# Block 1's second-half filter spectra from dense tables instead of two staged transforms, fewer guard matmuls, and a new written-out order

## The chip, the cores and the metric

The kernel runs on one core of a Trainium2 chip. The metric is the device time of one execution in microseconds (us); lower is better. The kernel before takes 278.72 us, the median of three runs (278.42 to 279.31).

## The reference

Two layers in a row on a sequence of 2048 positions with 640 channels. The first is a gated long convolution: the keys pass a short filter of four taps, are multiplied by the values, and the product is convolved along the sequence with a filter as long as the sequence. The second is a SwiGLU feed-forward layer.

```python
def _A_ref(q, k, v, shift_k, ssm_k, ssm_D):
    k_shift = sum(k_pad[:, t:t + S, :] * shift_k[:, ks - 1 - t] for t in range(ks))
    kv = k_shift * v
    y = irfft(rfft(kv, 2 * S) * rfft(ssm_k, 2 * S))[:, :S]      # per channel, causal
    y = y + kv * ssm_D
    return q * y

def _B_ref(x, w_gate, w_up, w_down):
    return (silu(x @ w_gate) * (x @ w_up)) @ w_down              # 640 -> 1728 -> 640

h = A_q + _A_ref(layernorm(A_q), A_k, A_v, A_shift_k, A_ssm_k, A_ssm_D)
out = h + _B_ref(layernorm(h), B_w_gate, B_w_up, B_w_down)
```

## The kernel before, in words

The sequence is cut into four blocks of 512 positions (j = 0 to 3), and the 640 channels into two column halves of 320 (c = 0 and 1). The convolution is done block by block through spectra of 1024 points. For each block and half the kernel needs a spectrum of the data (X) and a spectrum of the filter piece (K); products of these spectra are summed over the pairs of blocks that contribute, and the sum goes back to positions.

A spectrum is made in one of two ways.

- **Staged** (`fwd` at L659 and `spec` at L741): a first stage of 4 groups of 2 matmuls, 320 columns each, with 128x128 tables from the tile `tab` (names s1...); 4 evacuations by ScalarE (e1...); 4 transfers on SyncE's queue that exchange partitions (sh...); then a second stage of 4 groups (h = 0 to 3) of 4 small matmuls each, on a quarter of the array (64 by 64), which work side by side in pairs (s2...); and 4 more evacuations (e2...).
- **Dense** (`dense_h` at L689): 4 groups of 8 full matmuls of 320 columns with tables from the tile `den` (df...), and 4 evacuations (de...), with no transfer between.

Block 0 is all dense. Of the later blocks the set `DFW` says which spectra are dense: before, only the filter of block 1 in the first half, `("K",1,0)`. The dense tables lie in SBUF where the weights of the down projection (`wd`, and its last half tile `wdl`) are loaded later.

After the convolution of a block, VectorE and ScalarE form h (w..., h...), GpSimd takes the root of the variances (L878), the normed rows (hn...) are transposed (for block 0 by TensorE at L1143, names tr; for the others by DMA), and the feed-forward layer of that block runs on TensorE: gate and up (gu..., 5 matmuls of 512 or 256 columns in a group), silu on ScalarE (si..., L1198), a product on VectorE (gm...), and down (dn..., dl...) with the residual sum on VectorE (fa..., L1270 or L1251) and the store.

Nothing but data binds the order of the blocks: the feed-forward matmuls of one block fill TensorE while VectorE does the spectral products of the next (L751: m1, m2 products, ac sums, cr and ci combinations, kf filter sums, kvn, kva, kvv for the short filter). **The order is written out.** A packed table `_PLAN` gives for each operation its engine, its place in that engine's queue, its buffer slot, and extra ordering between transfers. `Prog.plan` reads it and `Prog.emit` issues each engine's list with semaphore waits where data or a buffer demands one. Each engine works strictly down its list, so an instruction that waits holds all behind it. All loads and exchanges but three stand in SyncE's one list.

TensorE also gets **guard matmuls**, on constant data and read by no one: `WARM` gives two sets (before, 5 and 4 matmuls of 512 columns) and `FILL` pairs of two (before, four pairs). Before, the first set and one pair stand at the very start; the second set and three pairs stand where block 0's convolution ends.

The tile `vin` holds the values of one block and half, loaded by SyncE into a single slot and multiplied in place (kvv). The key product of block 3's second half, kvv31, needs its load, vin31.

Of the kernel before, what the change touches and what calls it, by code (L numbers as in the profile page):

```python
# [317 lines left out]
def bass_sequential_preLN__ssm_conv_h3__swiglu_ffn__prompt_kernel(  # L318
# [20 lines left out]
    WARM = [5, 4]  # L339
    FILL = [2] * 4  # L340
# [10 lines left out]
    DFW = {("K",1,0)}  # L351
    KDMA = [[False, False], [True, True], [True, True], [True, True]]
    FM = 1664
# [12 lines left out]
    P = Prog()  # L366
    with ExitStack() as es:
# [335 lines left out]
        nks, dens = {}, []  # L703
# [603 lines left out]
        for j in range(NB):  # L1307
            block_j(j)

# [11 lines left out]
    "c-rlI2Y3@#*7m)URjgt)%a$$4vTRw!mYZa`$yS$Txy!v5Y~vDo?=28IgoIu~htL8E9YP=>VPPSmgiauY7FrT|Xd&ORu)z>^zukTIdv^cl&&)HPnS0MY=RNOv@67OUML<MEa39#c6H&`XfCINX+BPEc_y>2~x)a)6"  # L1321
    "wL~Gb`hOnb^*Fe-mGHvyAH92i{l~xmnTUiJ*%DqEMQpWeY4iAp_t!Vvn#aHI?)kMxyIw-OxPR~ZU)Mo<Cfgq`vwm5d*X#89*nicY@In!UKUn{7xc*!4zT_0U`S$o5t^a?j=kHa?<8Si*CjS3c-@nJx|CJK|+jIO!"
    ")JynNz5m2B=AVDc{O6yG|5upXbMDc4ys7n%Z&<>=;rexDwMBXv@t<!YxWCZ|?Y?AMGHLlPBOx;UB_bWPCZJ@L<nAZCEf~;FN1kBgfmn!wxQK>0h>5%r8!1tW`<ezle#i&$kT3FwRu8vN3Zla934U6xX>i2=Pi*7`"
    "KDcm2g^?T>>5ur(#sH7LNPt9ec*7omBq$ICAt89>BN+-oa-?#%MnTj-WJDI|jYWw_inPcE{>k8v<+k>OcyvG{1pjQXm4Qt#;1i%Q6p6x-23mZfUyUMAG>QS=L2x8M-g;z!D8Udb8JUp@S-~a}rJ)QM<v>obPeti~"
    "AQR=HY?OrxQ2}IEipo(1j7>&4C?6H0BEV9Ks==QD_Hgjdhmjia)WWR^+RWfN2Rvnfhg?8!L^Y@mT2r9c?)KpVFLsoN21Bm}Vq0NPK|Nqp2I_!1LhLFu3DBgWX4C}8I-vJaH`E1nLT|x+Bl-Z90fri|DuJu9s5|P9"
    "`haZ@v;^Acp^@kvGzLvXyHIB|9F0R0z}sgqdNO(!O-0kt9@G^LLPOCA7`qvKQh`|?U{nnC5<$KEfX!fFO#(HE0*+fynjnKA5VIO`DFPo9sHzuKfD0po-Qy%k0UiS2N(?oTLmd>btAL|u$T$yb5s%`arX`R=Eo9LE"
    "kz0^Az+FAy&I7ARsCNsS^^lhl_C#Q(GwKO=yP;lyc>rLpgNoEbO)`PY9^hjE^eu#*zUV`+T;$F}3Xwx0o)#iTf%c=_(e-d254q?;D{4Tf1e-AT-vl_T;Oqp}Gog0<&_K{Y1|W$=!+@#Y;Qehh3XKL<djq1*P^A*!"
    "p#n6L1tW$7<K<A<SnxCk7#|6ok4Nvh`R)nK_k!vbgO&zEotA@#rQme{S_9dyL@UrLXdj3^hB|D7{2IYq16qqdaYx<)ir)_Ynjk_m`Uq@WdKRF?=w~z&YW*QxO-6IkMew@>Z3Ej`VDl?jEQ0!f0m}Ip{RUND4+_`~"
    "u{IzAo&)v^(R@(Fd+01+`5Y866TJQoEf}9hKcGwK3X<Uk=rB5pj-ivt8_z|j&>3_NeUAe1eDqgz03AdpkPrR<W?KyK8w)Ha0^4ffqZ|}l3reYiOnac|z`?tqm<teb9iUu`p2CdQfvw#=GrB<KTjom|%oi8%nd?@*"
# [81 lines left out]
```

## Time and profile before

| | before |
|---|---|
| median of three runs | 278.72 us |
| the profiled execution, its own time | 278.8 us |
| its span, first to last instruction | 277.0 us |
| TensorE busy | 270.7 us, 98% |
| VectorE busy | 227.1 us, 82% |
| ScalarE busy | 196.7 us, 71% |
| DMA, mean over the span | 148 GB/s |

Times below are microseconds from the start of the span. PE is TensorE's matmul, PEld its weight loads, DVE is VectorE, ACT ScalarE, POOL GpSimd, SP SyncE (SPq its transfer issues). Ends of matmuls are modelled and overlap the next one's start, so the price of a matmul is taken from start to start. A bracket at the end of a row gives the idle time of the engine before it and what ended it.

### The profile page before, as it was taken

How to read it: one execution, taken by the hardware profiler on the slowest of the kernel's cores; microseconds unless marked ns; L12 is line 12 of the kernel's file. 1: busy time of each engine (PE TensorE's matmuls, PEld its weight loads, DVE VectorE, ACT ScalarE, POOL GpSimd, SP SyncE). 2: the span in 40 equal slices, each digit the busy share in tenths (PEclk: the TensorE clock that was granted, in tenths of full speed). 3: DMA queues.
4: the chain of work that ended last, by engine and by line, in shares of the span. 5: the costliest groups of instructions: out<-in, count | busy, mean ns of one | idle time of the engine just before them, and what ended most of it. 6: DMA issues, size and time to landing. Idle time of an engine off the chain costs nothing.

```text
span 277.0 us, 4869 instructions
## 1 busy us (share of the span) xinstructions
PE 270.7 (98%) x1761; PEld 149.3 (54%) x1761; DVE 227.1 (82%) x420; ACT 196.7 (71%) x319; POOL 13.1 (5%) x21
## 2 busy tenths in 40 slices
PE   8999999999999999999999999999999999999995
PEld 3676666454643575544444666444445766444573
DVE  3999999999999999999999998999997553015414
ACT  3479869999999988769998887879998730620000
POOL 1000200200001002000001011000001020000000
PEclk9999999999999999999999999999999999999999
DMA  6959969999889554665522645562021133000003
GB/s 191 282 162 294 223 178 262 271 225 300 294 244 252 198 142 122 193 211 146 164 68 80 193 133 140 161 200 84 23 74 55 50 62 106 12 0 0 0 14 107
DMA packets 54573, 40.97 MB, mean 148 GB/s; under 512 B 20243, under 2 KB 51732, under 8 KB 54550
## 3 DMA queue, kind: packets, MB, share of 16 engines
q1 hardware_dynamic: 54402, 40.63, 51.4%
q8 instruction: 14, 0.23, 0.3%
q14 instruction: 9, 0.07, 0.1%
q10 hardware_dynamic: 148, 0.04, 0.1%
HBM read 19.42 MB, written 2.62 MB: 80 GB/s over the span
## 4 chain that ended last, share of the span: by engine, by line
PE 50%; DVE 26%; ACT 8%; DMA 6%; SPq 4%; issue 3%; POOL 1%; DVEq 0%; ACTq 0%
PE ps L519 50%; DVE sb L751 23%; SPq L507 4%; DMA sb<-in_A_k_dram 3%; ACT sb L499 3%; DMA sb<-in_A_v_dram 2%; ACT sb L1097 1%; ACT sb L1198 1%; DMA sb<-sb 1%; POOL stt L878 1%; ACT sb L914 1%; DVE sb L1101 1%; DVE sb L1270 1%; ACT L1198 0%; ACT sb L893 0%
## 5 line engine op out<-in xcount | busy, mean ns | idle before, releaser
L519 PE MATMUL ps<-sb 128*128 128x320 bf16 (+3 forms) x1309 | 231.3, 332 | 1.5 <-DVE sb L533 1.1
L751 DVE TENSOR_TENSOR sb<-sb 128x1280 bf16<-128x1280 bf16 (+5 forms) x264 | 174.1, 721 | 2.4 <-DMA sb<-in_A_v_dram 1.0
L519 PEld LDWEIGHTS ps<-sb 128*128 128x128 bf16 (+2 forms) x1309 | 122.3, 98 | 96.0 <-issue 10.8
L499 ACT ACTIVATE sb<-ps 128x640 bf16<-128x640 f32 (+2 forms) x157 | 110.0, 755 | 24.7 <-PE ps L519 21.1
L519 PE MATMUL ps<-sb,tab 128*64 128x320 bf16 (+2 forms) x408 | 50.6, 302 | 1.9 <-DMA sb<-sb 0.8
L1198 ACT ACTIVATE sb<-ps 128x1024 bf16<-128x1024 f32 (+2 forms) x32 | 28.9, 918 | 19.3 <-PE ps L519 18.9
L519 PEld LDWEIGHTS ps<-sb,tab 128*64 128x64 f16 (+2 forms) x408 | 23.8, 101 | 26.6 <-issue 11.6
L751 DVE TENSOR_TENSOR sb<-ps,sb 128x1024 bf16<-128x1024 f32 (+3 forms) x18 | 15.8, 891 | 19.9 <-ACT sb L1198 15.4
L878 POOL TENSOR_TENSOR stt<-stt 128x2 f32<-128x2 f32 (+1 forms) x12 | 12.2, 1015 | 212.0 <-DVE stt L877 171.3
L1101 DVE SCALAR_TENSOR_TENSOR sb<-sb,stt 128x320 bf16<-128x320 bf16 x32 | 16.8, 543 | 5.5 <-ACT sb L1097 5.3
L1097 ACT ACTIVATE sb<-ps,stt 128x320 f32<-128x320 f32 x32 | 18.1, 619 | 4.3 <-PE ps L519 3.5
L921 ACT ACTIVATE sb<-sb,stt 128x640 uint8<-128x640 bf16 x16 | 13.2, 828 | 0.7 <-DVE stt L917 0.6
L1251 DVE SCALAR_TENSOR_TENSOR sb<-ps,stt,sb 128x320 bf16<-128x320 f32 x8 | 3.9, 546 | 10.4 <-PE ps L519 10.3
L1270 DVE SCALAR_TENSOR_TENSOR sb<-ps,stt,sb 128x640 bf16<-128x640 f32 x12 | 10.3, 877 | 2.5 <-PE ps L519 2.5
L914 ACT ACTIVATE sb<-sb 128x640 uint8<-128x640 bf16 x16 | 11.8, 735 | 0.3
L939 ACT ACTIVATE sb<-sb,stt 128x640 uint8<-128x640 bf16 x12 | 9.9, 826 | 0.9 <-DVE stt L934 0.7
L893 ACT ACTIVATE sb<-sb,stt 128x640 bf16<-128x640 bf16 x8 | 7.2, 914 | 0.7 <-DVE stt L885 0.7
L861 DVE BATCH_NORM_STATS2 stt<-sb 128x6 f32<-128x320 bf16 x8 | 3.8, 482 | 0.0
L892 DVE TENSOR_SCALAR sb<-sb,stt 128x640 bf16<-128x640 bf16 x8 | 3.4, 441 | 0.3 <-PE ps L1143 0.2
L500 DVE CAST sb<-ps 128x640 bf16<-128x640 f32 x1 | 0.8, 825 | 3.1 <-PE ps L519 3.1
L646 PE MATMUL ps<-sb 128*128 128x128 bf16 (+1 forms) x24 | 3.2, 226 | 0.0
L921 ACT ACTIVATION_READ_ACCUMULATOR sb<-sb,stt 128x1 f32 x16 | 3.1, 196 | 0.0
(24 smaller groups left out, 23.3 us busy)
## 6 DMA issues: line engine op xcount, KB each, us to landing
sb<-sb SPq DMA_DIRECT2D x68, 160.0 KB, 2.9
sb<-in_A_k_dram SPq DMA_DIRECT2D x6, 560.0 KB, 4.7
sb<-in_A_v_dram SPq DMA_DIRECT2D x8, 320.0 KB, 4.1
sb<-in_A_q_dram SPq DMA_DIRECT2D x8, 320.0 KB, 3.5
sb<-cst_den SPq DMA_DIRECT2D x8, 256.0 KB, 4.1
sb<-sb SPq DMA_DIRECT2D x24, 80.0 KB, 2.5
out_dram<-sb SPq DMA_DIRECT2D x12, 160.0 KB, 2.0
sb<-in_B_w_down_dram SPq DMA_DIRECT2D x3, 480.0 KB, 5.1
```

The source lines that it names most:

```text
L499: fns = {"act": lambda a: a.activation(out=dst(), in_=src(), func=ACTF.Copy), "dve": lambda v: v.tensor_copy(out=dst(), in_=src())}
L507: fns = [(lambda g, d=d, s=s: g.dma_start(d(), s())) for d, s in subs]
L519: return lambda t: t.matmul(o(), l(), r(), start=st, stop=sp)
L751: return lambda v: v.tensor_tensor(out=o(), in0=a(), in1=b_(), op=op)
L878: P.op({"pool": 1.05}, lambda g: g.tensor_tensor(out=y, in0=va, in1=stt[:, oCO + 4:oCO + 4 + hi - lo], op=ALU.pow), c1 + [(ST, "half")], c ...
L914: P.op({"act": act_c(D) + 0.22}, lambda a, b=b, jt=jt: a.activation(out=JU(jt), in_=V(xt, b * D, D), func=ACTF.Copy, accum_out=tmv(l, j, 4 ...
L921: P.op({"act": act_c(D) + 0.3}, lambda a, b=b, jt=jt: a.activation(out=JU(jt), in_=V(xt, b * D, D), func=ACTF.Square, bias=tmv(l, j, 5)[:, ...
L939: P.op({"act": act_c(D) + 0.3}, lambda a, b=b, jt=jt: a.activation(out=JU(jt), in_=V(xt, b * D, D), func=ACTF.Square, bias=tmv(l, j, 5)[:, ...
L1097: P.op({"act": act_c(CW, True)}, lambda a, k=k, b=b, wt=wt: a.activation(out=VF(wt, CW), in_=B32(pt, k, CW), func=ACTF.Identity, scale=tmv ...
L1101: vec(dve1(CW), lambda v, b=b, wt=wt, xv=xv: v.scalar_tensor_tensor(out=xv(), in0=xv(), scalar=tmv(0, j, 5)[:, b:b + 1], in1=VF(wt, CW), o ...
L1198: P.op({"act": act_c(n)}, lambda a: a.activation(out=dst(), in_=src(), func=ACTF.Silu), rd, wr, -1000, name=f"si{j}{i}")
L1270: vec(dve1(640), lambda v: v.scalar_tensor_tensor(out=hv(), in0=B32x2(pt, CW), scalar=tmv(0, j, 5)[:, b:b + 1], in1=hv(), op0=ALU.subtract ...
```

## The change

Three things change. The filter of block 1's second half becomes dense too; the second guard set (4 matmuls) and two of the four guard pairs go; and `_PLAN` is a new table, so that nearly every queue has a new order. A loop is added that makes the loads `wd` and `wdl` wait for every dense matmul of blocks 0 and 1, since these read the tables that lie where those weights go.

```diff
-    WARM = [5, 4]
-    FILL = [2] * 4
+    WARM = [5, 0]
+    FILL = [2] * 2
...
-    DFW = {("K",1,0)}
+    DFW = {("K",1,0),("K",1,1)}
...
         for j in range(NB):
             block_j(j)
+        for o in P.ops:
+            if o.name in ("wd", "wdl"):
+                for d in dens:
+                    if d not in o.deps:
+                        o.deps[d] = 2
+                        d.succ.append(o)
+                        o.npred += 1
...
 _PLAN = (
-    "c-rlI2Y3@#*7m)URjgt)%a$$4vTRw!mYZa`$yS$Txy!v5Y~vDo?=28IgoIu~htL8E9YP=>VPPSmgiauY7FrT|Xd&ORu)z>^zukTIdv^cl&&)HPnS0MY=RNOv@67OUML<MEa39#c6H&`XfCINX+BPEc_y>2~x)a)6"
...
+    "c-rlI2Xs@%y7i1?S(2?{HCvWt6-$<7xk|Dv*(z4CY{|CVd&9V!-a{y%*H8i>5J(7w4xt7@XbAyQfDj111_FfMLJ6JlJ_{2ZC-?pL-al)-`_{`j>zp%Z%2)Q@b2MHI1Vlsx&xJiF5w#q+-G!ju>z_Pv>q%%+YOzo7"
```

The engines' lists differ in these operations. TensorE loses 8 first-stage matmuls, 16 small second-stage matmuls and 8 guard matmuls of 512 columns, and gains 32 dense ones, so the count stays at 1761. ScalarE loses the four evacuations of the first stage. SyncE loses four exchanges. Two operations change engine, both from VectorE to ScalarE: the first evacuation of the taps at the start (L500 before), and one normed row of block 2 (hn23, L892 before, L893 now).

The first place is on TensorE, at the end of block 0's convolution. Before, from the last 8 inverse matmuls of block 0 (the first 8 of row 32; its other 24 are three dense groups of the first half's filter) to the first of the two transposes at L1143. `sb,tab 64x320` are second-stage groups, `sb,tab 128x320` first-stage matmuls, `sb 128x512` guards:

```order
32 L519 MATMUL ps<-sb 128x320 x32
33 L519 MATMUL ps<-sb,tab 128x320 x4
34 L519 MATMUL ps<-sb,tab 64x320 x4
35 L519 MATMUL ps<-sb,tab 128x320 x2
36 L519 MATMUL ps<-sb,tab 64x320 x4
37 L519 MATMUL ps<-sb 128x512 x4
38 L519 MATMUL ps<-sb,tab 64x320 x8
39 L519 MATMUL ps<-sb,tab 128x320 x2
40 L519 MATMUL ps<-sb 128x512 x2
41 L519 MATMUL ps<-sb,tab 64x320 x4
42 L1143 MATMUL ps<-sb 128x128 x10
```

Of the change, the same place; the last 8 inverse matmuls are the third group of eight in row 30, with dense groups before and behind them, and rows 32, 34, 36 and 39 are dense groups:

```order
30 L519 MATMUL ps<-sb 128x320 x40
31 L519 MATMUL ps<-sb,tab 64x320 x8
32 L519 MATMUL ps<-sb 128x320 x8
33 L519 MATMUL ps<-sb,tab 64x320 x8
34 L519 MATMUL ps<-sb 128x320 x8
35 L519 MATMUL ps<-sb,tab 64x320 x4
36 L519 MATMUL ps<-sb 128x320 x8
37 L519 MATMUL ps<-sb 128x512 x2
38 L1143 MATMUL ps<-sb 128x128 x10
39 L519 MATMUL ps<-sb 128x320 x16
40 L1143 MATMUL ps<-sb 128x128 x10
```

Dense groups of eight now stand between the second-stage groups and between the two transposes, where guards and first-stage matmuls stood.

The second place is block 3's filter in the first half. On SyncE, before, from a 64x512 transfer of block 1 (the only one there) to the load of vin31 (`in_A_v_dram`); `128x1x640` are exchanges, `32x4x320` pieces of the next filter:

```order
114 L507 DMA sb<-sb 64x512
115 L507 DMA sb<-sb 128x1x640
116 L507 DMA sb<-sb 32x4x320
117 L507 DMA sb<-sb 128x1x640
118 L507 DMA sb<-in_A_v_dram 128x4x320
```

Now, from the same transfer to the same load:

```order
110 L507 DMA sb<-sb 64x512
111 L507 DMA sb<-sb 32x4x320
112 L507 DMA sb<-sb 128x1x640
113 L507 DMA sb<-sb 32x4x320
114 L507 DMA sb<-sb 128x1x640
115 L507 DMA sb<-sb 32x4x320
116 L507 DMA sb<-sb 128x1x640 x4
117 L507 DMA sb<-sb 32x4x320
118 L507 DMA sb<-in_A_v_dram 128x4x320
```

Row 117 of before, and rows 114 and 116 of now but for one transfer, are exchanges of that filter; the load stood behind one of them, and now stands behind all four and seven transfers in all, counted from row 114.

On TensorE at that place, before, `sb,tab 128x320` are the filter's four first-stage pairs (row 123, row 125, the last two of row 129) and inverse matmuls, the others down projections of block 1:

```order
122 L519 MATMUL ps<-sb 128x320 x10
123 L519 MATMUL ps<-sb,tab 128x320 x2
124 L519 MATMUL ps<-sb 128x320 x10
125 L519 MATMUL ps<-sb,tab 128x320 x4
126 L519 MATMUL ps<-sb 128x320 x6
127 L519 MATMUL ps<-sb,tab 128x320 x4
128 L519 MATMUL ps<-sb 128x320 x10
129 L519 MATMUL ps<-sb,tab 128x320 x6
```

Now the four pairs are rows 119 and 121:

```order
118 L519 MATMUL ps<-sb 128x320 x10
119 L519 MATMUL ps<-sb,tab 128x320 x4
120 L519 MATMUL ps<-sb 128x320 x10
121 L519 MATMUL ps<-sb,tab 128x320 x4
122 L519 MATMUL ps<-sb 128x320 x6
```

The filter's last pair now ends 28 matmuls behind the start of that first down group, and stood 52 behind it before.

The third place is on VectorE, where kvv31 stands. Before it is row 199; the row behind it is hn23:

```order
195 L1270 SCALAR_TENSOR_TENSOR sb<-ps,stt,sb 128x640
196 L751 TENSOR_TENSOR sb<-sb 128x1280
197 L885 TENSOR_TENSOR stt<-stt 128x2
198 L877 TENSOR_SCALAR stt<-stt 128x2
199 L751 TENSOR_TENSOR sb<-sb 128x1280
200 L892 TENSOR_SCALAR sb<-sb,stt 128x640
```

Now kvv31 is the first of row 200:

```order
192 L1270 SCALAR_TENSOR_TENSOR sb<-ps,stt,sb 128x640
193 L877 TENSOR_SCALAR stt<-stt 128x2
194 L751 TENSOR_TENSOR sb<-sb 128x1280 x2
195 L885 TENSOR_TENSOR stt<-stt 128x2
196 L1270 SCALAR_TENSOR_TENSOR sb<-ps,stt,sb 128x640
197 L877 TENSOR_SCALAR stt<-stt 128x2
198 L751 TENSOR_TENSOR sb<-sb 128x1280 x2
199 L885 TENSOR_TENSOR stt<-stt 128x2
200 L751 TENSOR_TENSOR sb<-sb 128x1280 x4
```

Three products of 1280 columns (one in row 194, both in row 198) that stood behind kvv31 now stand ahead of it.

More of the change, by code (lines that the diff above doesn't have):

```diff
@@ new lines @@
+    "*m?29t@rj9q4h-n!rP1TAMgJ&9tpo?OZeR=Vr##aI<J5FY=7X^JpQ`37iF(Dt%Npy|GV<PuY<Now!L0u{fe9RJhdPD@AfDBrU=3xdjF@z^$I)e!PV;@)c)U8$$!U^*FVJl&+z|8ZGVlW{~yKuZ_e>=_5Qoe{$n=&"
+    ")vwH7`~CY*in%T3Uai-k)&B99l<*gn+bip(r&k{T^&0HS`em*!E@JEYiv%YbT6FM^k+)}EMuU1^M1@`?#DG>7@<AL#M?B<*WYCiiHNJ?6{Go<}1c(o{ULJd7M1gS>u+wt-K-m}W3>fE+0>LiLQ)YR_(V@&nLZ}yk"
+    "1s0U~C<v@c;Lb)|BuAl0ft1iHLt12kvK6HuDKa1j^ofBuS|VqHJuX;l@#+Jm7C%B1g2JFr2nqmODinbtQ5@Lg!Fx1{La|5#?J}^fM~Ns28KI99yqS<0B_kX3jzMWC6RA-;a>IyJ<b*LUl!0<l4k|?X;JFx;qH-8-"
```

114 lines of the change are left out of this document (55 added, 59 removed).

## The prediction

> **What bounds the kernel now.** I read the page's busy shares first, then its slices, to see which engines have room, and where.
>
> ```profile
> PE 270.7 (98%) x1761; PEld 149.3 (54%) x1761; DVE 227.1 (82%) x420; ACT 196.7 (71%) x319; POOL 13.1 (5%) x21
> ...
> PE   8999999999999999999999999999999999999995
> ...
> DVE  3999999999999999999999998999997553015414
> ACT  3479869999999988769998887879998730620000
> ```
>
> PE is busy in every slice (each is a fortieth of the span, 6.9 us). DVE is as full as PE in the slices from the second to the thirtieth and then empties. So the share of 82% misleads: it is an average over a full stretch and an empty one. The stretches show it in us:
>
> ```profile
> 14.50:211.00 196.50, 194.10 (x1275) 104.03 (x1273) 193.41 (x357) 172.52 (x285) 9.38 (x9) 1.00 0.62 176
> ```
>
> In the 196.5 us from 14.5 to 211 PE is busy for 194.10 and DVE for 193.41 (first and third of the busy columns). PE idles 2.4 us there and DVE 3.1 us. **Two engines work down their lists side by side**, and either can hold the other. After 211:
>
> ```profile
> 211.00:277.00 66.00, 63.15 (x413) 37.68 (x411) 24.32 (x52) 17.99 (x29) 2.77 (x3) 1.00 0.15 43
> ```
>
> Here PE has 413 matmuls left and DVE is idle for two thirds. This last stretch is PE's own, and its end moves with the time at which PE gets to it. A change is worth what both lists lose ahead of 211, and where they lose unequally, the smaller of the two.
>
> Which short waits set the pace before 211? For that I looked for idle brackets on PE and DVE in the timeline.
>
> ```profile
> 43.20 4.52 PE L519 MATMUL ps<-sb 128*128 128x320 bf16 x32
> ...
> 47.55 0.71 PE L519 MATMUL ps<-sb,tab 128*128 128x320 bf16 x4
> ...
> 49.11 1.23 PE L519 MATMUL ps<-sb,tab 128*64 128x320 bf16 x10 [0.85 <-DMA sb<-sb]
> ...
> 63.90 0.46 PE L519 MATMUL ps<-sb,tab 128*64 128x320 bf16 x4 [0.47 <-ACT sb L1198]
> 64.29 1.25 PE L519 MATMUL ps<-sb 128*128 128x512 bf16 x5
> ...
> 65.29 0.82 DVE L751 TENSOR_TENSOR sb<-sb 128x1280 bf16<-128x1280 bf16 x1 [0.27 <-ACT sb L499]
> 65.40 0.43 PE L519 MATMUL ps<-sb,tab 128*128 128x320 bf16 x2
> ...
> 167.83 0.82 DVE L751 TENSOR_TENSOR sb<-sb 128x1280 bf16<-128x1280 bf16 x1 [0.95 <-DMA sb<-in_A_v_dram]
> 168.69 0.45 DVE L892 TENSOR_SCALAR sb<-sb,stt 128x640 bf16<-128x640 bf16 x1
> ...
> 168.71 0.72 PE L519 MATMUL ps<-sb,tab 128*128 128x320 bf16 x4 [0.45 <-DVE sb L751]
> ```
>
> PE waits 0.85 us for an exchange of block 1's second half, 0.47 for a silu that must free its PSUM, and 0.45 for kvv31, which itself waits 0.95 us on DVE for the load vin31. That is 1.77 of PE's 2.4 idle us.
>
> **The change, part by part.** The sum is made against the profiled execution, 278.8 us for a span of 277.0; the 1.8 us around the span are not touched. The median, 278.72, lies 0.1 below it.
>
> *PE's work.* A full matmul of 320 columns costs (47.55 - 43.20) / 32 = 0.136 us, one of 512 columns (65.40 - 64.29) / 5 = 0.22 us. A second-stage group of four, from 63.90 to 64.29, costs 0.39: two pairs side by side, 2 x 0.136 = 0.27, and 0.12 for the way back to full matmuls. Added: 32 x 0.136 = 4.35. Removed: 8 first-stage matmuls, 1.09; four groups of small ones, 4 x 0.27 = 1.09; 8 guards, 8 x 0.22 = 1.76. That alone is **+0.41 us**. But PE's list now has 20 stretches of small matmuls where it had 24. The way in costs little more:
>
> ```profile
> 72.80 1.24 PE L519 MATMUL ps<-sb 128*128 128x512 bf16 x5
> 73.97 0.81 PE L519 MATMUL ps<-sb,tab 128*64 128x320 bf16 x8
> ```
>
> Five matmuls of 512 took 1.17 ahead of small ones and 1.11 ahead of full ones, so 0.06. Four stretches fewer save 4 x 0.18 = 0.72, between nothing (if the new neighbours cost as much) and that. I take all of it, as the nearest rows have it. PE's own work: **-0.3 us**, bounds -0.3 and +0.4.
>
> *PE's waits at the first place.* The 0.85 us wait goes: at 49.11 PE had run out of dense groups, and now four more groups of eight (4.35 us) stand among the second-stage groups and the transposes. The 0.47 us wait for silu goes too, because ACT was the late engine there:
>
> ```profile
> 43.00:66.00 23.00, 21.69 (x154) 11.70 (x153) 22.41 (x45) 22.41 (x36) 1.45 (x2) 1.00 1.03 263
> ...
> 150.00:176.00 26.00, 25.33 (x190) 15.40 (x189) 24.36 (x52) 22.12 (x38) 2.77 (x3) 1.00 0.54 146
> ```
>
> ACT was busy for 22.41 of these 23 us (fourth busy column), and four first-stage evacuations leave it:
>
> ```profile
> 161.42 0.69 ACT L499 ACTIVATE sb<-ps 128x640 bf16<-128x640 f32 x1
> ...
> 166.84 0.92 ACT L893 ACTIVATE sb<-sb,stt 128x640 bf16<-128x640 bf16 x1
> ```
>
> 4 x 0.69 = 2.8 us is six times the wait. Late next is the normed row for the first transpose:
>
> ```profile
> 51.47 0.80 DVE L892 TENSOR_SCALAR sb<-sb,stt 128x640 bf16<-128x640 bf16 x2
> ```
>
> From the last inverse matmuls (done by about 44.3: the first 8 of the 32 at 43.20) to the end of these two norms, 52.3, the chain took 8.0 us. PE's new list holds 5 dense groups, 5 small ones and a guard pair in between, 5 x 1.09 + 5 x 0.27 + 0.44 = 7.2 us and its turns. So up to 0.8 us of the 0.85 can come back as a wait for DVE; then DVE's list decides, which is counted next.
>
> *DVE's list.* It loses hn23, 0.45 us (the row at 168.69). ACT takes it at 0.92 (the row at 166.84), in a stretch where it is free for 3.9 of 26 us, and the transfer behind it is wanted by the feed-forward of block 2 only. DVE loses the tap evacuation too, but ahead of waits that stay:
>
> ```profile
> 4.80 0.82 DVE L500 CAST sb<-ps 128x640 bf16<-128x640 f32 x1 [3.12 <-PE ps L519]
> 5.81 4.57 DVE L751 TENSOR_TENSOR sb<-sb 128x2560 bf16<-128x2560 bf16 x4 [0.18 <-DMA sb<-in_A_k_dram]
> ...
> 14.56 1.89 DVE L751 TENSOR_TENSOR sb<-sb 128x2560 bf16<-128x2560 bf16 x2 [0.66 <-DMA sb<-in_A_k_dram]
> ```
>
> The load of the keys ends both waits, so **0** there (at most 0.18). Up to 14.56 the new list does the same work, and from there DVE is full. The 0.27 us wait at 65.29 was for a second-stage evacuation of the first half; its group now stands ahead of the transposes, so it goes. The 0.95 us for vin31 is the large one. The load was issued behind one exchange:
>
> ```profile
> 162.14 0.54 SPq L507 DMA_DIRECT2D sb<-sb  x1
> 162.79 0.58 SPq L507 DMA_DIRECT2D sb<-in_A_v_dram  x1
> ...
> 169.05 1.55 DVE L751 TENSOR_TENSOR sb<-sb 128x1280 bf16<-128x1280 bf16 x2
> ```
>
> That exchange waited for the filter's last first-stage evacuation, 161.42 to 162.11 on ACT; the load came at 162.79 and kvv31 ran at 167.83, 5.04 us later. Now the filter's last pair ends 28 matmuls behind the first down group and not 52, so 24 x 0.136 = 3.3 us earlier, and the evacuation ends near 158.8. Seven transfers of about 0.6 us follow, 158.8 + 4.3 = 163.1; but the table also makes SyncE hold the load until the fourth of them, an exchange of 160 KB, has landed, 2.9 us by its row below: 158.8 + 3 x 0.62 + 2.9 = 163.6, and data 5.04 later, 168.6. On DVE three products, 3 x 0.78 = 2.3 us, now stand ahead of kvv31, so that it is wanted not at 167.83 - 0.95 = 166.9 but near 169, with the 0.27 off. The load is there about 0.4 us early, and the wait goes. DVE's list ahead of 211: 0.45 + 0.27 + 0.95 = **1.67 us** less. PE's first stage of that half waits for kvv31, and its 0.45 goes with it.
>
> *SyncE's list.* Four exchanges go (0.6 us of issue each). The new waits of `wd` and `wdl` hold that queue once: one `wdl` load stands ahead of the pieces of block 2's filter and now waits for the last dense group, between the two transposes, near 55. The rows of exchanges and of such pieces on the page:
>
> ```profile
> sb<-sb SPq DMA_DIRECT2D x68, 160.0 KB, 2.9
> ...
> sb<-sb SPq DMA_DIRECT2D x24, 80.0 KB, 2.5
> ```
>
> Four of them issue in 2.4 us and land 2.5 later, near 61; PE's list has 40 matmuls of 512 and 30 of 256 columns, 40 x 0.22 + 30 x 0.11 = 12 us, between the second transpose and the first use, so near 67. Cost **0**; without that cover it would be what the issue is late beyond 6 us.
>
> *The guards.* In no stretch above does the granted clock fall below 1.00 (the column ahead of the DMA share), and PE idles 1.3 us in all between 43 and 66. At the start PE does run at half pace:
>
> ```profile
> 1.46 0.15 PEld L519 LDWEIGHTS ps<-sb 128*128 128x128 bf16 x1 [0.28 <-issue]
> 1.88 0.15 PEld L519 LDWEIGHTS ps<-sb 128*128 128x128 bf16 x1 [0.28 <-issue]
> ...
> 4.87 0.13 PEld L519 LDWEIGHTS ps<-sb 128*128 128x128 bf16 x1 [0.16 <-issue]
> 5.16 0.12 PEld L519 LDWEIGHTS ps<-sb 128*128 128x128 bf16 x1 [0.16 <-issue]
> ```
>
> A guard takes 0.42 us there, not 0.22, and a tap matmul of 320 columns 0.29 at 4.87, not 0.136. These first guards stay. Those that go stood between real matmuls, and dense matmuls take their place, so I cost their loss at nothing; the cover is that PE stays fed. [...]
>
> *The sum.* PE could gain 0.3 + 0.85 + 0.47 + 0.45 = 2.1 us, DVE 1.67. Both lists are full up to 211, so the smaller counts: 1.67. Of that I give back 0.3 for waits that a new order brings of its own. The old order has such:
>
> ```profile
> 97.29 0.55 DVE L1101 SCALAR_TENSOR_TENSOR sb<-sb,stt 128x320 bf16<-128x320 bf16 x1 [0.34 <-ACT sb L1097]
> ...
> 164.12 0.88 DVE L1270 SCALAR_TENSOR_TENSOR sb<-ps,stt,sb 128x640 bf16<-128x640 f32 x1 [0.33 <-PE ps L519]
> ```
>
> One of this size is what I add. **1.4 us less: 278.8 - 1.4 = 277.4 for the profiled execution, 277.3 us for the median.**
>
> **The rivals.**
>
> *The waits change place only.* DVE's waits come back elsewhere, vin31's or another of its size: the gain is hn23 and the 0.27, 0.7 us, so 278.0. For it: PE and DVE are so close that any late step costs both. Against it: each of the four waits named has lost its cause.
>
> *The load vin31 comes late; slower.* In the new list it stands behind all four exchanges of the filter. If the filter's last evacuation ends not near 158.8 but as late as before, at 162.1, the load is issued at 162.1 + 1.9 + 2.9 = 166.9, and kvv31 runs at 171.9. In the old list, with the three products ahead of it, it would have run at 167.83 + 2.3 = 170.1. That is 1.8 late, less the 0.7 gained: 278.7 + 1.1 = 279.8. It decides for slower once that evacuation ends after about 161.8. For it: seven more places in the queue. Against it: 24 matmuls less ahead of the evacuation.
>
> *The clock falls at the first place.* If PE drops to half pace there for as long as at the start (by the rows at least from 1.46 to 5.16, 3.7 us; I take 4.5), half of that is lost: 277.3 + 2.3 = 279.6. [...]
>
> *The dense spectrum does not pay and nothing else moves.* Then PE's own work counts, +0.4 at most: 279.1.
>
> **How the numbers follow.** A run of this kernel can be told from no change at about 0.3%, 0.84 us. My forecast, 277.3, has a chance of 0.58; its own range is from 276.4 (PE's whole 2.1 us and a little of its small waits) to 277.9. The waits that change place, 278.0, have 0.20; the late load, 279.8, 0.12; the clock, 279.6, 0.03; no gain, 279.1, 0.07. The range goes from 276.1, for the rest of PE's 2.4 idle us, to 279.5, which leaves out the late load, the clock, and a few in a hundred below. Faster by over 0.3% (under 277.9) are the forecast but for its edge and a little of the first rival: 0.59. Within 0.3% lie most of the first rival and the case of no gain: 0.26. Slower: 0.15.
>
> **What would show it.** Right: no bracket over 0.3 on PE between 43 and 66 and none near 168; the load from in_A_v_dram near 163.6 and DVE without a wait for it; in the stretch to 211 DVE idle for about 2 us and PE's tail of 66 us unchanged in length. Wrong: a PE wait for a norm (L892) ahead of the first transpose that is longer than 0.8; matmuls of 320 columns at more than 0.136 us in a stretch around 50; DVE idle for 3 us or more before 211, with new releasers. If DVE's idle time fell and PE still ended as late, the claim that the smaller gain counts would be wrong.

## The result, and the profile after

The changed kernel takes **281.64 us** (median of four runs, 280.85 to 283.11) where before took 278.70 beside it: a ratio of 1.0117 with a 95% interval of 1.0089 to 1.0145, so it is slower by 2.9 us. Two later sets of runs gave 282.49 us (ratio 1.0147, 1.0123 to 1.0171) and 282.19 us (1.0129, 1.0099 to 1.0158). The forecast was 277.3.

The profiled execution took 280.85 us, the fastest of the four, with a span of 279.0. First the page's busy shares and two stretches. Sixteen matmul records are missing (x1745 of 1761), so PE's busy time is too low by some 2 us; the weight loads (PEld) are complete.

```profile
PE 268.3 (96%) x1745; PEld 150.8 (54%) x1761; DVE 226.4 (81%) x418; ACT 195.3 (70%) x317; POOL 14.0 (5%) x21
...
q8 instruction: 14, 0.23, 0.4%
q14 instruction: 9, 0.07, 0.1%
```

```profile
14.50:211.00 196.50, 189.81 (x1253) 104.78 (x1264) 191.39 (x353) 167.86 (x279) 10.19 (x9) 1.00 0.62 173
...
43.00:66.00 23.00, 21.64 (x166) 13.15 (x167) 21.79 (x45) 20.21 (x31) 2.02 (x2) 1.00 0.99 243
```

DVE is idle for 196.50 - 191.39 = 5.1 us up to 211, where it was 3.1. ACT, busy for 22.41 of the 23 us from 43 to 66 before, has 2.8 us free now, and the waits are still there: it was not ACT's work that the first place lacked.

The idle brackets say where. These are the timelines of PE, ACT and DVE of the changed kernel at the places that matter.

```profile
50.58 1.25 PE L519 MATMUL ps<-sb 128*128 128x320 bf16 x8 [1.20 <-ACT sb L499]
...
91.49 0.45 PE L519 MATMUL ps<-sb,tab 64*128 64x320 bf16 x4 [0.70 <-ACT sb L499]
...
169.06 1.53 PE L519 MATMUL ps<-sb 128*128 128x320 bf16 x10 [1.03 <-ACT sb L499]
```

```profile
90.41 1.62 ACT L499 ACTIVATE sb<-ps 128x1024 bf16<-128x1024 f32 x2 [1.09 <-DVE sb L751]
...
113.20 0.92 ACT L893 ACTIVATE sb<-sb,stt 128x640 bf16<-128x640 bf16 x1 [1.50 <-DMA sb<-sb]
...
168.31 0.70 ACT L499 ACTIVATE sb<-ps 128x640 bf16<-128x640 f32 x1 [1.97 <-DMA sb<-sb]
```

```profile
54.53 0.45 DVE L892 TENSOR_SCALAR sb<-sb,stt 128x640 bf16<-128x640 bf16 x1 [0.61 <-PE ps L1143]
...
122.47 12.60 DVE L751 TENSOR_TENSOR sb<-sb 128x1280 bf16<-128x1280 bf16 x19 [0.67 <-DMA sb<-sb]
...
169.85 0.17 DVE L877 TENSOR_SCALAR stt<-stt 128x2 f32<-128x2 f32 x1 [1.16 <-ACT sb L939]
171.52 0.15 DVE L885 TENSOR_TENSOR stt<-stt 128x2 f32<-128x2 f32 x1
171.59 3.43 DVE L751 TENSOR_TENSOR sb<-sb 128x1280 bf16<-128x1280 bf16 x5
```

None of the four waits that the prediction named is left: no exchange at 49, no silu at 64, no 0.27 at 65, and kvv31, the first of the row at 171.59, starts without a bracket. In their place PE waits 1.20 us at 50.58 for the first dense group, and ACT and PE wait for a transfer near 168. The row at 50.58 names ACT; three more profiles (of the runs e3, e14 and e16), two of them quoted below, show the same group with a transfer named. It is the fourth piece of the filter, `shk11` (a filter piece is copied into its tile in four transfers of 80 KB, `shk`, and a dense group reads all four). On SyncE:

```profile
42.15 0.59 SPq L507 DMA_DIRECT2D sb<-in_B_w_gate_dram  x1
42.78 1.21 SPq L507 DMA_DIRECT2D sb<-sb  x2
44.70 0.38 SPq L507 DMA_DIRECT2D sb<-in_A_k_dram  x1
45.13 1.49 SPq L507 DMA_DIRECT2D sb<-sb  x2
```

The piece is the first of the two at 45.13, right behind a load of 560 KB; the load itself had waited for its buffer. In before it was issued at 41.79. In the changed kernel it landed at 50.34, 0.4 us behind the load, and the group that reads it starts at 50.58, 5.45 us after the issue; the transfer engines are full there (the DMA share of 0.99 in the stretch above). That the row names ACT does not matter: in all seven profiles with this gap (three of the changed kernel, and those of e3, e9, e14 and e15 below) the group starts 0.24 to 0.25 us after this piece has landed.

The transfer near 168 is the last of the thirteen in the first row here, issued at 164.44, with vin31 behind it. It is the last piece of the filter of block 3's second half, `shk31`. It landed at 168.20, and the ACT row at 168.31 follows it:

```profile
156.20 8.85 SPq L507 DMA_DIRECT2D sb<-sb  x13
165.16 0.59 SPq L507 DMA_DIRECT2D sb<-in_A_v_dram  x1
```

**An account of PE.** I took as a wait each gap between two weight loads beyond what the matmuls between them take, and summed from 11 us on.

| kernel | span | PE's waits | span less waits |
|---|---|---|---|
| before | 277.0 | 4.8 | 272.2 |
| changed, first profile | 279.0 | 7.4 | 271.6 |
| changed, second | 280.5 | 8.5 | 272.0 |
| changed, third | 280.0 | 8.2 | 271.8 |

By this count PE's own work fell by 0.2 to 0.6 us, and all the loss is waits: the order that came with the change brings 2.6 to 3.7 us more of them than it removes. The count is good to some 0.4 us between two lists of matmuls (further down it finds 1.4 and 1.5 us for guards worth 1.76), so the waits are clear of doubt, but not the sign of PE's own work.

### The profile page after: what moved, and what is told of

It reads as the page before. It is cut to its first block, busy times and chain, and to the rows that moved or that the text cites. A ratio compares the mean times of both kernels' runs of the same rounds, so it can differ in the third digit from the quotient of the medians.

```text
span 279.0 us, 4839 instructions
## 1 busy us (share of the span) xinstructions
PE 268.3 (96%) x1745; PEld 150.8 (54%) x1761; DVE 226.4 (81%) x418; ACT 195.3 (70%) x317; POOL 14.0 (5%) x21
## 4 chain that ended last, share of the span: by engine, by line
PE 55%; DVE 21%; DMA 10%; ACT 7%; issue 4%; SPq 2%; ACTq 0%; DVEq 0%
PE ps L519 54%; DVE sb L751 21%; DMA sb<-sb 5%; ACT sb L499 4%; DMA sb<-in_A_k_dram 3%; DMA sb<-in_A_v_dram 2%; SPq L507 2%; ACT sb L893 1%; ACT sb L1097 1%; ACT sb L939 1%; ACT sb L1198 0%; PE ps L1143 0%; ACT sb L914 0%; DVE sb L1251 0%; ACTq L227 0%
## 5 line engine op out<-in xcount | busy, mean ns | idle before, releaser
L519 PEld LDWEIGHTS ps<-sb 128*128 128x128 bf16 (+1 forms) x1333 | 125.1, 98 | 98.7 <-issue 11.9
L499 ACT ACTIVATE sb<-ps 128x640 bf16<-128x640 f32 (+2 forms) x154 | 108.3, 758 | 25.6 <-PE ps L519 18.6
L519 PE MATMUL ps<-sb,tab 128*64 128x320 bf16 (+2 forms) x384 | 47.1, 302 | 2.2 <-ACT sb L499 1.2
L519 PEld LDWEIGHTS ps<-sb,tab 128*64 128x64 f16 (+2 forms) x384 | 22.4, 101 | 24.5 <-issue 9.0
L878 POOL TENSOR_TENSOR stt<-stt 128x2 f32<-128x2 f32 (+1 forms) x12 | 13.0, 1082 | 213.1 <-DVE stt L877 213.1
L893 ACT ACTIVATE sb<-sb,stt 128x640 bf16<-128x640 bf16 x9 | 8.1, 913 | 1.5 <-DMA sb<-sb 1.5
L892 DVE TENSOR_SCALAR sb<-sb,stt 128x640 bf16<-128x640 bf16 x7 | 3.0, 445 | 1.4 <-DMA sb<-sb 0.7
L914 ACT ACTIVATION_READ_ACCUMULATOR sb<-sb 128x1 f32 x16 | 3.2, 201 | 0.0
```

The source lines that it names most:

```text
L499: fns = {"act": lambda a: a.activation(out=dst(), in_=src(), func=ACTF.Copy), "dve": lambda v: v.tensor_copy(out=dst(), in_=src())}
L519: return lambda t: t.matmul(o(), l(), r(), start=st, stop=sp)
L878: P.op({"pool": 1.05}, lambda g: g.tensor_tensor(out=y, in0=va, in1=stt[:, oCO + 4:oCO + 4 + hi - lo], op=ALU.pow), c1 + [(ST, "half")], c ...
L893: "act": lambda a: a.activation(out=dst(), in_=src(), func=ACTF.Identity, scale=rs(l, j, b), bias=tmv(l, j, 3)[:, b:b + 1])},
L914: P.op({"act": act_c(D) + 0.22}, lambda a, b=b, jt=jt: a.activation(out=JU(jt), in_=V(xt, b * D, D), func=ACTF.Copy, accum_out=tmv(l, j, 4 ...
```

## The experiments

Theory O: the new order of transfers causes the loss. Rivals: the dense spectrum costs more than worked out, or the missing guards do. Every ratio below is against before on the same chip.

**e1 and e16: the changed kernel again.** 

> The changed kernel once more, unaltered, as the yardstick for the runs beside it and for the spread of its times (280.85 to 283.11 in four runs). Theory O (the order causes the loss): the same waits stand at the same places whatever the run, so about 281.5 us, and the profile again shows PE waiting over 1 us for the first of the dense groups of block 1's second half near 50.6 and ScalarE about 2 us near 168. Rival L (the landing of transfers decides from run to run): those two waits differ by more than 0.5 us from the first profile, and the span with them.

> The changed kernel unaltered, beside these three on the same chip: 281.5 to 282.5 us, a load between 110 and 112, the waits of 1 us and more near 50.6, 91, 115 and 169 as before, and granted clocks of 0.994 in a part of its runs.

Measured: 282.49 and 282.19 us. The wait for the fourth piece, by the count of the table, was 2.0 and 2.4 us (1.35 in the first profile), that at the down group near 169 1.0 in both (1.3). So both theories have a share: the order sets the places, and the landing of the piece varies by up to 1 us. In 5 of all 15 runs of this kernel the mean granted clock was 0.993 or 0.994, and these are the five slowest, 283.04 to 283.34; the other ten average 281.8. Of 95 runs of before beside these and the later ones, one has such a clock.

**e2, e3, e4: filter pieces issued earlier.** Only SyncE's list is changed:

```diff
         P.plan(_PLAN)
+        sp = P.order["sp"]
+        for a, b in ((42, 38), (142, 141), (147, 142)):   # e2: the first; e3: the others; e4: all
+            o = sp.pop(a)
...
+            sp.insert(b, o)
```

> The changed kernel with one transfer moved on SyncE: the fourth piece of the filter of block 1's second half (shk11) is issued in the place of the gate weights wg03, ahead of the exchanges and of the load kin21, where it stood behind that load. It should issue near 42 in place of 45.1. Theory A (every wait on PE adds to the end): the wait of about 1.3 us at the first dense group goes, and the time falls by 1.0 to 1.4 us against the changed kernel. Theory S (the smaller saving of the two lists counts, as the prediction had it): DVE also waited 0.6 us there for the first transpose, and no more than that 0.6 us is won. Theory N (the wait moves to the next late thing): under 0.3 us.

> The changed kernel with two transfers moved on SyncE: the third and fourth pieces of the filter of block 3's second half (shk31) are issued ahead of the four exchanges of the first half's filter, in the 0.5 us that SyncE waits there for ScalarE. ScalarE waited 1.97 us for the last of them (its buffer holds the raw filter until all four have read it), PE 1.3 us and DVE 1.2 us behind it. Theory A: 1.0 to 1.4 us less than the changed kernel. Theory S: the smaller of PE's and DVE's waits, about 1.2 us less, so here the two agree. Theory N: under 0.3 us, because the exchanges of K30 or the load vin31 are then late instead.

> Both moves of the two runs before. Theory A: 2.0 to 2.8 us less than the changed kernel, so 278.7 to 279.5, about the kernel before. Theory S: 1.8 us less, 279.7. Theory N: under 0.6 us less. If the two effects add to within 0.4 us, the waits are independent places on one path.

Measured: 279.96 us (ratio 1.0063, 1.0044 to 1.0082), 279.96 us (1.0064, 1.0038 to 1.0089), and both 278.69 us (1.0007, 0.9988 to 1.0025). Against e1 beside them that is 2.5, 2.5 and **3.8 us** less. With both moves the kernel is level with before. In e4's profile PE's waits are 4.9 us in sum, and neither the bracket at 50.6 nor that at 169 is there. PE at both places, then DVE from kvv31 on:

```profile
48.82 0.73 PE L519 MATMUL ps<-sb,tab 128*64 128x320 bf16 x8
49.50 1.25 PE L519 MATMUL ps<-sb 128*128 128x320 bf16 x8
...
168.83 0.71 PE L519 MATMUL ps<-sb,tab 128*128 128x320 bf16 x4
169.37 1.22 PE L519 MATMUL ps<-sb 128*128 128x320 bf16 x8
```

```profile
169.94 3.42 DVE L751 TENSOR_TENSOR sb<-sb 128x1280 bf16<-128x1280 bf16 x5
```

Theory O holds for these 3.8 us. e4 lies at the lower end of theory A's range; theory S allowed 0.6 us for e2 and 1.8 for e4, and falls short. The gain of one move was above every theory's, and the two add to 1.3 us less than their sum, so they are not independent places on one path. e2's bound of 1.4 came from the first profile's wait, the mildest of the three of the unaltered kernel. In e2's own profile part of the wait has only moved, to an exchange that a small group (`128*64`: these work on 128 rows by 64 columns, half of the array and not a quarter) waits for:

```profile
56.87 0.46 PE L519 MATMUL ps<-sb,tab 128*64 128x320 bf16 x4 [1.01 <-DMA sb<-sb]
```

Why each single move still gains 2.5 us, the profiles do not show.

e3 caught the other cost of the late piece. Its PE timeline around the wait, and the stretches with the granted clock (the column ahead of the DMA share):

```profile
51.15 2.12 PE L519 MATMUL ps<-sb 128*128 128x320 bf16 x8 [2.29 <-DMA sb<-sb]
53.20 0.74 PE L519 MATMUL ps<-sb,tab 128*64 128x320 bf16 x4
53.87 2.12 PE L519 MATMUL ps<-sb 128*128 128x320 bf16 x10
```

```profile
48.00:50.00 2.00, 0.85 (x10) 0.37 (x8) 1.98 (x10) 2.00 (x5) 0.81 (x1) 1.00 1.12 324
50.00:52.00 2.00, 0.85 (x5) 0.52 (x6) 1.43 (x7) 0.43 (x1) 1.20 (x2) 0.84 0.38 89
52.00:54.00 2.00, 2.00 (x10) 0.75 (x9) 1.39 (x1) 0.01 (x1) 0.00 (x0) 0.50 1.01 339
54.00:56.00 2.00, 2.00 (x14) 1.22 (x13) 0.00 (x0) 2.00 (x4) 0.00 (x0) 0.81 1.12 292
```

After 2.29 us of idling the clock is 0.50 (the stretch from 52 to 54), and eight matmuls take 2.12 us where the same row took 1.25 above. Means of 0.84, 0.50 and 0.81 over three stretches of 2 us are, if the clock is taken as either full or half, 0.64, 2.00 and 0.76 us at half, 3.4 us in sum, an estimate. In e16 the gap was a little shorter, and the clock stayed at 1.00 (from 48 to 56):

```profile
51.76 1.25 PE L519 MATMUL ps<-sb 128*128 128x320 bf16 x8 [2.21 <-DMA sb<-sb]
```

Whether the 0.08 us between the two gaps made the difference, or where each gap lay, no run shows. Over all runs with the piece late and the gap open (e1, e3, e9, e14, e15, e16 and the first four) 11 of 61 have a mean clock of 0.995 or less; with the piece early (e2, e4, e10, e11, e12) none of 47.

**e5, e6, e7: the change's parts in the old order.** The plan of before was carried over by names. For e5 the four dense groups stand where the filter's first-stage groups stood, and the guards stay; e6 takes the guards too; e7 is before with the guards taken.

```diff
-    WARM = [5, 4]
-    FILL = [2] * 4
+    WARM = [5, 0]
+    FILL = [2] * 2
...
-    DFW = {("K",1,0)}
+    DFW = {("K",1,0),("K",1,1)}
```

> The order of before with the dense filter alone: the four dense groups stand where the four first-stage groups of that filter stood, their evacuations where those evacuations stood, its four exchanges and four second-stage groups are gone, and all guards of before are kept. Work on PE by the prediction's terms: +4.35 - 1.09 - 1.09 - 0.72 = +1.45 us. The 0.85 us wait for an exchange at 49.1 and the 0.47 us wait for a silu at 63.9 should go. Theory W (PE's work and its waits add up): 0.1 us above before, with anything up to +1.4 if the waits come back elsewhere. Theory D (the dense spectrum itself is what costs in the changed kernel): +2 us or more, as there. If it is near before, the changed kernel's loss lies in its order.

> The run before with the guards taken out as in the changed kernel (the set of four and two of the three later pairs; one pair ahead of the first transpose is kept), so the whole content of the change in the old order. PE's own work is -0.3 us against before by the prediction's terms. Theory W (PE's work and waits add up): about 1.4 us faster than before, 276.8. Theory S (the smaller saving of PE's and DVE's lists counts): DVE's list loses only its 0.27 us wait, so 0.3 us faster, 277.9. Theory D (the dense spectrum costs): slower than before. Theory C (guards hold the clock): granted clocks of 0.99 in some runs and a wider spread of times.

> The kernel before with the same guards taken out and nothing else: eight matmuls of 512 columns less, 1.76 us of PE's work. The norms for the second transpose come at 54.4 in before, 0.1 us ahead of the transpose, so PE should mostly wait where the guards stood: 0 to 0.3 us faster than before by theory W. Theory C (guards hold the clock): a granted clock of 0.99 in some runs, and a median above before.

Measured: e5 280.19 us (1.0072, 1.0057 to 1.0088), e6 279.90 (1.0062, 1.0044 to 1.0080), e7 279.99 (1.0043, 1.0015 to 1.0071, runs from 277.32 to 281.25). Theory W missed all three. By its own terms theory D came out in e6 (slower than before) and nearly in e5 (1.87 us slower, where it said 2 or more): in the old order the kernel with the dense spectrum is the slower one. In the changed kernel the spectrum is not the loss, since e4 has the same matmuls and is level with before. The account of the three:

| kernel | span | PE's waits | span less waits |
|---|---|---|---|
| e5 dense, guards kept | 278.6 | 4.3 | 274.3 |
| e6 dense, guards out | 278.1 | 5.3 | 272.8 |
| e7 guards out alone | 277.7 | 6.9 | 270.8 |

By the count e5's own work is 2.1 us above before, not 1.45. The 0.72 us for four fewer turns is hardly earned in the old order: PE's list has 24 stretches of small second-stage matmuls in before and 20 in the changed kernel, but 23 in e5 and 22 in e6. Without it the terms give 1.45 + 0.72 = 2.17. e6 is 0.6 above before, near the bound of +0.4. And the waits that the dense groups remove return: both have a new one behind the feed-forward's start.

```profile
67.24 0.43 PE L519 MATMUL ps<-sb,tab 128*128 128x320 bf16 x2 [0.83 <-ACT sb L499]
```

(This is e5; e6 has the same 0.83.) e7's work fell by 1.4 us, nearly the 1.76 of the guards, but waits of 2.1 us came, at the places of the guards and, in this profile, far from there for an exchange of block 3:

```profile
188.97 0.89 PE L519 MATMUL ps<-sb,tab 128*64 128x320 bf16 x8 [1.17 <-DMA sb<-sb]
```

All of e7's runs have a clock of 0.999 or more: in the old order the guards do not hold the clock. What they cost by going is then not the clock. The next runs show a second thing that a change in the number of instructions does, and these three have it too: a load of instructions at 111.1, 110.5 and 109.9 among the transposes of block 1's normed rows, where before has none, and ACT waits of 0.45, 0.44 and 0.78 us for a transfer behind it. So their distance from before is not the dense spectrum's or the guards' alone.

**e8: the wait filled.** Ten idle dense matmuls ahead of the late group.

```diff
+            idle = [mm(lambda: B32(pt, 0, CW), lambda: den(0), lambda: V(TAPS, 0, CW), True, True)] * 10 if (r + nm, h) == ("X10", 1) else []
-            pe(stage2(u, h, pt), CW, 2, ...
+            pe(idle + stage2(u, h, pt), CW, 2, ...
```

> The changed kernel with ten idle dense matmuls of 320 columns (1.36 us, their result is written over) put ahead of the small group that stands before the first dense group of block 1's second half, so that PE works for most of the 1.3 to 2.4 us that it waited there. Transfers are as in the changed kernel. Theory C (in part of the runs of the changed kernel the gap lets the clock fall, and that costs a further 0.8 to 1.3 us): no run with a granted clock below 0.998, the slowest runs go, the median 0.2 to 0.5 us below the changed kernel beside it (282.5). Rival R (the low clock of such runs comes from elsewhere): granted clocks of 0.994 in two runs of five as before, median unchanged. If the wait was shorter than 1.36 us, the filling costs up to 0.3 us.

Measured: 279.73 us (1.0064, 1.0042 to 1.0085), no run under a clock of 0.999. The clock part held, as far as six runs can tell, and the gain against e1 (2.8 us by the medians, 2.3 by the ratios) is more than four times what theory C allows: 1.36 us of added work made the kernel faster. In its profile the dense group still starts at 50.6; the time is won later, near 114, 122, 154 and 168. There ACT's 1.50 us wait is gone, and so is something in the transfer queues. Here are the queues of the changed kernel between 108 and 114 (the second row is GB/s in 40 slices):

```profile
GB/s 0 0 0 0 0 0 0 0 0 0 0 0 53 220 224 213 212 142 24 114 0 0 94 217 215 205 126 15 7 10 12 10 177 3 1 0 0 0 41 210
DMA packets 1492, 0.38 MB, mean 64 GB/s; under 512 B 1491, under 2 KB 1491, under 8 KB 1491
...
q8 instruction: 1, 0.02, 1.2%
...
sb<-sb SPq DMA_TRANSPOSE x3, 3.4
```

Three transposes of normed rows run there, and one load of 16 KB on the queue q8, which holds instructions (14 loads on the page above, 0.23 MB in all). Behind the second burst of traffic comes a tail of five slices at 7 to 15 GB/s and one last slice of 177, up to 112.95. The norm at 113.20, the fourth, writes over the row that the first of the transposes reads. That one was issued at 108.68 and landed at 113.11, 4.4 us later. The median to landing is 3.4 us; in e8 none of q8's loads falls there, and it is 2.6.

**e9, e14, e15: the same shift without the filling.** Short matmuls behind the first guards move PE's instructions along and leave the gap at 50 alone.

```diff
             fns = [mm(lambda: ps[:, pt.base:pt.base + 512], lambda: V(w, 0, 128), rhs, True, True)] * n
+            if w is ONE:
+                fns = fns + [mm(lambda: ps[:, pt.base:pt.base + 16], lambda: V(w, 0, 128), lambda: V(w, 0, 16), True, True)] * 10   # e14: 5, e15: 20
```

> The changed kernel with ten matmuls of 16 columns added to the first guards, near 2.7 us, where PE idles 0.57 us anyway. The run with the filled wait was 2.7 us faster than the changed kernel, more than its gap and clock explain; its profile has no load of instructions between 108 and 114 us, where the changed kernel has one while the normed rows of block 1 are transposed and ScalarE waits for them, and the same loads move by several us elsewhere. This run moves PE's instructions by the same twenty places and leaves the gap as it is. Theory I (where PE's instruction loads fall among the transfers decides 1 to 2 us): 280.0 to 281.0 us, and no load between 108 and 114. Theory C (the filled gap and its clock did it): 282.0 to 282.5, as the changed kernel.

> The changed kernel with five short matmuls at the start in place of ten. Theory I: the load at 110.9 moves by about half as far as with ten or by a whole step; if the profile shows none between 108 and 114, the time is near 279.1 as with ten, and if one is left there, near 282. Rival G (the amount of added work helps): half of the gain, 280.7, whatever the loads do.

> The changed kernel with twenty short matmuls at the start. Theory I: again the place of the loads decides, near 279.1 if none falls between 108 and 114, plus up to 0.3 us for the added work, and 281 to 282 if the next one has come into that stretch. Rival G: at or below the run with ten, 279.

Measured, with the time of q8's load nearest to those transposes (the first of which is issued between 108.2 and 109.9 in the profiles of this table):

| kernel | q8's load at | ACT's wait for a transfer at the fourth norm | median |
|---|---|---|---|
| changed | 110.9 | 1.50 | 281.64 |
| changed, third set (e16) | 112.1 | 1.32 | 282.19 |
| e14, five | 106.5 | none | 280.46 |
| e9, ten | 104.0 | none | 279.13 |
| e15, twenty | 103.2 | none | 279.66 |
| e8, ten elsewhere | 104.9 | none | 279.73 |

The ratios are 1.0058 (1.0036 to 1.0081) for e14, 1.0024 (1.0006 to 1.0043) for e9 and 1.0047 (1.0023 to 1.0070) for e15. These loads are PE's: with ten matmuls more on PE this one moves by 6.9 us, while q14's load at 114.5 stays at 114.4. e9's queues in the same stretch, for comparison:

```profile
GB/s 0 0 0 0 0 0 0 0 0 36 208 227 217 212 164 29 0 0 0 72 213 224 213 213 144 14 0 0 0 17 183 220 215 213 197 48 0 0 36 210
...
sb<-sb SPq DMA_TRANSPOSE x4, 2.6
```

and SyncE's four transposes, first of the changed kernel, then of e9:

```profile
108.68 6.67 SPq L1135 DMA_TRANSPOSE sb<-sb  x4
```

```profile
108.24 5.57 SPq L1137 DMA_TRANSPOSE sb<-sb  x4
```

So one load among the transposes makes ACT's norm late by 1.5 us and the row of the four transposes longer by 1.1, and SyncE's list behind is held with it. That much is shown beyond these two: in the seven profiles of the changed order with a load there (the three of the changed kernel, e2, e3, e4 and e11) the first transpose lands 4.2 to 4.5 us after its issue and ACT waits 1.3 to 1.5 us; in the six without (e8, e9, e10, e12, e14, e15) it lands after 2.6, and ACT waits for no transfer there.

That the load's place decides the whole gain is not shown. e9 gained more than theory I allowed (279.13, where it said 280.0 to 281.0). Theory C fails, as e9 still has the gap. e15, 279.66, is nearer to theory I (279.1 and up to 0.3 for the added work) than to rival G (279 or less). But e14 has no load between 108 and 114, and came out at 280.46: rival G said 280.7, theory I 279.1. No row of PE quoted here shows it waiting for a load of q8; the transfers beside the load are late (4.2 to 4.5 us for the first, 2.6 without). That the wait at 122 and those of 0.3 to 0.8 us near 150 come from the late list and from the load at 148.3 is argued, not shown: e14, with a load at 147.2, keeps 0.84 us near 154, and e9, e8 and e15 (145.7 to 146.5) have 0.5 to 0.6.

**e13: is before favoured?** The same ten short matmuls in before. 

> The kernel before with the ten matmuls of 16 columns added to its first guards. Its loads of PE's instructions fall at 106.5 and 124.3, none while the four normed rows of block 1 are transposed. Theory I with before favoured: the shift brings a load among transfers that are waited for, 278.7 becomes 279.5 or more. Theory I without: within 0.4 us of before. Rival G (the short matmuls help by themselves, by an earlier full clock at the start): 1 us or more below before.

Measured: 279.21 us (1.0022, 0.9999 to 1.0045), between the two forecasts of theory I. The difference of 0.6 us is not clear of noise (from nothing to 1.3), so it is not shown that before is favoured; if it is, by a small part of the 3 us that the changed kernel gains by the same edit. Rival G fails here: in before the short matmuls are no help by themselves. Its earlier full clock is not shown either: in before the granted clock is 1.00 in each stretch of 2 us from 0 to 8.

**e10, e11, e12: what the change gives once its order is mended.** e10 has both moves of e4 and the ten short matmuls. e11 has both moves and two products earlier on DVE, since ACT waits 1.09 us for the second of them, gm03, at 90.41. e12 has all.

```diff
+        dve = P.order["dve"]
+        dve[146:150] = [dve[i] for i in (148, 149, 146, 147)]
```

> The changed kernel with both moves on SyncE (278.7 before) and the ten short matmuls at the start. Theory I: the waits of 0.4 and 0.3 us near 114 go, and part of the 0.8 near 154: 277.7 us, 1.0 less than without. Theory C: no change, 278.7, since no gap is left there.

> The changed kernel with both moves on SyncE, and on DVE the two products ci112 and gm03 put ahead of kvv21 and va01. In the changed kernel ScalarE waits 1.2 us for gm03 near 89 and PE 0.9 to 1.4 us behind it at the last inverse groups of block 1. Theory A (each wait on PE adds): 0.9 to 1.2 us less, 277.6. Theory S (DVE's list decides, and DVE did not wait there): no change, 278.7.

> All of these together: both moves on SyncE, the two products early on DVE, ten short matmuls at the start. Theories A and I together: 276.7 us, 0.5% faster than before and 0.6 below the forecast of 277.3, with PE's waits from 11 us on near 3.0 us in sum where before has 4.8. If DVE's list decides, no gain beyond the run before it.

Measured: e10 **277.09 us** (0.9946, 0.9923 to 0.9968), e11 278.08 (0.9974, 0.9955 to 0.9993), e12 **276.72 us** (0.9934, 0.9915 to 0.9954). PE's waits are 3.6, 4.7 and 2.8 us; e12's span of 274.7 less 2.8 is 271.9, the changed kernel's own work. e10 gained more than theory I's 277.7, and e12 lies where theories A and I together had it. e12's stretch up to 207, two us ahead of its tail, and the last wait that the swap left there:

```profile
14.50:207.00 192.50, 189.99 (x1256) 105.02 (x1268) 191.08 (x354) 168.94 (x280) 10.54 (x9) 1.00 0.63 177
```

```profile
89.94 0.45 PE L519 MATMUL ps<-sb,tab 64*128 64x320 bf16 x4 [0.29 <-ACT sb L499]
```

DVE idles 1.4 us of it, where the changed kernel idled 5.1. e12 beats both kernels, before by 0.7%. The swap alone is worth 0.4 us by the medians (0.3 by the ratios) from e10 to e12, and 0.6 (0.9) from e4 to e11. The intervals overlap, so between A and S it decides nothing.

## Why the prediction was wrong

**PE's own work, -0.3 us: not contradicted.** The account gives -0.2 to -0.6, good to some 0.4. The 0.72 us for four fewer turns hangs on the new neighbours: e5 and e6 have one and two fewer, not four.

**The waits of 0.85 and 0.47 go: right, and beside the point.** Both went. The norm that was to be late next was not; DVE even waited 0.61 us for PE at the first transpose. The prediction asked which engine would be late and went through PE, ACT and DVE; late was a transfer.

**DVE's list, -1.67: the three terms are right, the total is not.** hn23 moved, the 0.27 and the 0.95 are gone. The load vin31 was issued at 165.16, not 163.6, and still nothing waited for it. In the changed kernel that is partly because all else there was late; in e4, with the late pieces out of the way, it was issued at 164.54, and kvv31 at 169.94 did not wait either. But DVE's idle time rose from 3.1 to 5.1 us.

**SyncE's list at no cost: wrong.** This is one failed step. The prediction followed two transfers through that list, wdl and vin31, and not those that the same list moved behind others: the last pieces of two filters. One stands behind a load that waits for a buffer; the other became the last ahead of vin31, and it holds a buffer that ScalarE must write. Moving them forward in SyncE's list gives 3.8 us. The other part of this term was right: the `wdl` load that waits for the dense groups cost nothing that shows, as PE has no bracket over 0.2 us between 58 and 91.

**The guards at no cost: half wrong.** The cover named was that PE stays fed. With the late piece it is not: in 5 of 15 runs the clock fell, and those runs are about 1.4 us slower than the others; with e8's filling there is none in 6, with the early piece none in 47. The rival of the clock had 0.03 and a price of 4.5 us at half pace, both the author's estimates. No run shows from which length on a gap lets the clock fall, and none shows the 4.5. PE's gap ahead of the first dense group was 1.20, 1.81 and 2.21 us in the three profiles of the changed kernel, with the clock at 1.00 from 48 to 56, and 2.29 in e3, with the 3.4 us at half; the longest near there in before was 0.85.

**The sum: the 0.3 us for "waits that a new order brings of its own" is the term that was mis-sized.** Before's 4.8 us of waits lose 2.3 at the three places on PE by the same count, which leaves 2.5; the changed kernel has 7.4 to 8.5. The new order brought 5 to 6 us of its own: 1.4 to 2.4 for the first piece, 1.0 to 1.3 for the second, 1.0 for gm03, 0.7 for the transposes near 114, and the rest in smaller ones. The first rival had the mechanism, that waits change place, but with 0.7 us of gain left over. That the smaller saving of two lists counts was not put to the test for the sum, since DVE's list came out longer; at the places of e2 and e4 it failed, with 2.5 and 3.8 us gained where it allowed 0.6 and 1.8. That PE's last stretch keeps its length held: from the row of 16 inverse matmuls at 211.18 (213.21 in the changed kernel, 208.91 in e12) to the end of the span it is 65.8 us in all three.

What stands is that the content can be worth what was said: with two transfers and the instruction loads out of the way, e10 takes 277.09 us, 0.2 from the forecast. That closeness is in part luck, since e10's order is not the one forecast and its waits are others. Of the distance from the changed kernel (282.5, 282.2) to e10, 3.8 us are the two pieces and 1.6 the short matmuls, taken in this order; the other way round it is 3.1 for the short matmuls and 2.0 for the pieces. How the 2 to 3 us that the short matmuls gain without the moves divide among single waits stays open, as each kernel has one profile only.

## What to carry to other kernels

Where a change brings a new written-out order, go through the transfer list as closely as through the engines': for each transfer moved behind another, ask what it waits behind, who reads it and which buffer it frees. A new order costs waits of its own that no row of the old profile shows. In this one case they were 5 to 6 us against 2.3 removed, so price them as a range that reaches as far as what is removed and beyond, not at one small wait. Where a time changes by 1% for no reason in the work, look where the instruction loads fall among short transfers before blaming an engine: here seven profiles of the changed order with such a load among the transposes had ACT waiting 1.3 to 1.5 us behind them, and six without it had no such wait.

## What the hardware showed that was not expected

- With one 16 KB load of PE's instructions among them, the transposes by DMA in the first profile of the changed kernel landed 3.4 us after their issue (median; the first after 4.4); in e9, with none there, it was 2.6. Ten matmuls of 16 columns at the start moved it away, and the kernel went from 282.2 to 279.1 us; how much of that is the load's is not shown.
- Behind an idle gap of 2.29 us on PE (e3) the granted clock was 0.84, 0.50 and 0.81 in three stretches of 2 us, by the estimate above 3.4 us at half; behind one of 2.21 us in another profile (e16) it stayed at 1.00.
- An 80 KB transfer behind a 560 KB load, with the transfer engines full, landed 0.4 us behind the load and 5.2 us behind its own issue; the median to landing of its kind in before was 2.5.
